# An agent attention with two expert layers: routing of a group may begin earlier, and the order's estimate counts SyncE's time differently

## The chip, the cores and the metric

The kernel runs on one core of one Trainium2 chip. The core has TensorE for matmuls (PE in the rows), VectorE (DVE), ScalarE (ACT), GpSimd (POOL) and SyncE (SP), which here issues nearly all transfers. The metric is the device time of one execution, in microseconds (us), as the median over runs.

## The reference

There are 2 batches of 11456 rows with 128 channels. First comes agent attention: 49 agents attend to all keys of their batch, which gives a table of agent values, and each row's query attends to the 49 agents. Then two layers of experts follow, each with 8 experts of which a row takes one:

```python
def sm(a, b):
    s = scale * (a @ b.transpose(0, 2, 1))
    e = np.exp(s - s.max(-1, keepdims=True))
    return e / (e.sum(-1, keepdims=True) + 1e-09)
x = (sm(q, agents) @ (sm(agents, k) @ v)).reshape(B * S, D)

# layer 1: logits of normalised rows against normalised embeddings, / tau
# layer 2: logits = x @ w_gate
for each layer:
    expert_idx = argmax(logits); gate_w = softmax(logits)[expert_idx]
    h = relu(x[mask] @ w1[e])                       # 128 -> 1024
    out[mask] = gate_w[mask, None] * (h @ w2[e])    # 1024 -> 128
```

## The kernel before, in words

**Groups and units.** The rows of a batch are cut into 12 groups, 11 of 1024 rows and one of 192, so there are 24 groups, numbered 0 to 23. In a group most rows take one expert, the dominant one. The group as a whole goes through the dominant expert of layer 1, then through the dominant expert of layer 2. Rows that want another expert go onto lists and are done after the groups. The work of one layer on 512 rows is a unit. A unit has 8 steps, one per 128 columns of the hidden layer. Units of layer 1 of group i alternate with units of layer 2 of group i - 2; steps are counted through all units.

**A step.** TensorE makes the first product into PSUM (h), ScalarE writes relu of it as a 16 bit value (hh), VectorE writes the remainder (hl), and TensorE adds the second product to acc. In layer 1 the first product is two matmuls, h<-pt,slotG, with weights (slotG) that already hold the agent values times the expert's first matrix; the second is acc<-hh,slot2a twice and acc<-hl,slot2a once. In layer 2 it is h<-yh,slot1b twice, h<-yl,slot1b once, and three of acc with slot2b. There are 4 buffers for h (NH), so TensorE may have up to three steps of first products ahead of the second products.

**Between the layers.** The result of layer 1, acc, is split into yh (ScalarE) and yl (VectorE), turned by a transpose transfer (yr) and written to DRAM (R). For a group's routing, the queries are loaded (qt), cast by ScalarE and split by GpSimd (qs), multiplied by the agents on TensorE, put through a softmax on VectorE and ScalarE (sd, pr) and turned by a transpose transfer (pt). Some twenty small VectorE operations (lg, lwq, lm, oh, key, md, dom, ks, di) find each row's expert and the number di of the dominant one. SyncE reads that number into a register (value_load, TENSOR_LOAD in the order) and loads the weights it names (slotG, slot2a, later slot1b, slot2b). In the second batch the attention is computed from kt and vb in the same stretches; ScalarE casts them to ws.

**What sets the order.** Each engine runs its instructions in a fixed order, written when the program is built. A planner walks through the steps; class Clock (line 88 on) holds an estimate of when each engine is free and each tensor is written. Method note (line 126) prices an instruction: for a transfer the engine's own time, then the time of SyncE's transfers in line (hw) and the arrival; for a value_load the engine's time. Work besides the steps comes from chains, generators that start at a given step with a priority: chain_Q loads the queries of a group, chain_A does its first routing, chain_B the second, chain_S2 loads slots, chain_Z writes out results. Where an engine has room by the estimate, the planner places the next piece of a chain; time_L1 and time_L2 (line 2030 on) say when a first or a second product could go, and the earlier one is issued. So an estimate that changes moves instructions on every engine, and the chip then runs that order with its own times. s1 of a group is the step of its first unit; for group 3 and later it is 64 + 32 (i - 3).

Of the kernel before, what the change touches and what calls it, by code (L numbers as in the profile page):

```python
# [84 lines left out]
class Clock:  # L85
# [38 lines left out]
    def note(self, k, op, a, kw):  # L124
        ap = lambda x: type(x).__name__ == "AP"
        out = kw.get("out", a[0] if a else None)
        ins = [x for i, x in list(enumerate(a[1:])) + list(kw.items()) if ap(x) and i not in ("out", "accum_out")]
        outs = [x for x in (out, kw.get("accum_out")) if ap(x)]
        name = lambda x: x.tensor.name
        loc = lambda x: x.space != bass.MemoryType.DRAM and not name(x).startswith(("Sbig", "LF1", "LF2"))  # L130
        s = max(self.t, self.eng[k])
        for x in ins:
            if loc(x) and name(x) in self.wr:
                e, q = self.wr[name(x)]
                s = max(s, e + self.LAG[q])
        for x in outs:
            if loc(x):
                s = max(s, self.rd.get(name(x), 0.0))
        if "dma" in op:
            e = s + (1.05 if k == "pool" else 1.17 if "transpose" in op else 0.06)  # L140
            nb = min(x.nbytes() for x in outs + ins[:1])
            if k != "pool":
                self.hw = max(self.hw, s) + 0.47
            self.dma = max(self.dma, (e if k == "pool" else self.hw) + 0.65) + nb / 300e3 * (0.3 if "cond" in kw else 1.0)
            self.arr = self.dma + 1.0
            for x in outs:
                if loc(x):
                    self.wr[name(x)] = (self.arr, "dma")
            for x in ins:
                if loc(x):  # L150
                    self.rd[name(x)] = self.arr
            self.eng[k] = e
            return
        if op == "value_load":
            self.eng[k] = s + 0.1
            return
        both = sum(ap(x) and x.space not in (PSUM, bass.MemoryType.DRAM) for x in [kw.get(n) for n in ("in_", "in0", "in1")])
        if k == "dve" and (both > 1 or both == 1 and op in ("tensor_scalar", "tensor_copy") and outs[0].size() // outs[0].shape[0] > 1):

            for a_, b_ in self.held:  # L160
                if a_ <= s < b_:
                    s = b_
        self.start = s
        e = s + (0.3 + 0.16 * (outs[0].size() // outs[0].shape[0]) if kw.get("op") == ALU.pow else self.price(k, op, outs[0] if outs else None, ins or outs, kw))
        if k == "pool" and both > 1 and kw.get("op") != ALU.pow:
            self.held = self.held[-12:] + [(s, e)]
        for x in outs:
            if loc(x):
                self.wr[name(x)] = (e, k)
        for x in ins:  # L170
            if loc(x):
                self.rd[name(x)] = max(e, self.rd.get(name(x), 0.0))
        self.eng[k] = e
        self.end = max(self.end, e)
# [24 lines left out]
def agent_moe_kernel(ctx, tc, qT, kT, v, agT, embT, tau, wg, w1a, w2a, w1b, w2b, cst, out):  # L199
    nc = tc.nc  # L200
    clk = Clock()
    pe, act, dve, pool, sp = (Queue(clk, k, e) for k, e in (("pe", nc.tensor), ("act", nc.scalar), ("dve", nc.vector), ("pool", nc.gpsimd), ("sp", nc.sync)))
# [677 lines left out]
    def until(*keys):  # L880
        yield keys
# [22 lines left out]
    def c_S(g):  # L904

        tp, nt = g.tp, g.nt
        if g.i >= 1:
            yield from until(("S", g.i - 1))
        if g.i >= NS:
            yield from until(("Sx", g.i - NS))  # L910
        if g.i >= NR:
            yield from until(("A", g.i - NR))
        qs = qsp.tile([128, 2048], F16, name="qs", tag="qs")
        ql = qs.bitcast(BF16)
        n = g.n
        act.activation(out=qs[:, 0:n], in_=g.q[:, 0:n], func=AF.Copy)
        yield 1
        pieces(ql[:, 1024:1024 + n], g.q[:, 0:n], qs[:, 0:n], ALU.subtract, 4)
        done.add(("qs", g.i))
        yield 1  # L920
        k = yield "m"
        psv = misc(k)[0:tp, 0:nt * A].rearrange("p (t a) -> p t a", a=A)
        for t in range(nt):
            scores(psv[:, t, :], qs[:, t * tp:(t + 1) * tp], ql[:, 1024 + t * tp:1024 + (t + 1) * tp], g.b)
        done.add(("S", g.i))
        yield 1
        mx = sm.tile([128, 8], F32, name="smx", tag="smx")
        dve.tensor_reduce(out=mx[0:tp, 0:nt], in_=psv, axis=AX, op=ALU.max)
        g.sd = sdp.tile([128, 8, A], F32, name="sd", tag="sd")
        sdv = g.sd[0:tp, 0:nt, :]  # L930
        dve.tensor_tensor(out=sdv, in0=psv, in1=b3(mx, g, A), op=ALU.subtract)
        free(k)
        yield 2
        act.activation(out=sdv, in_=sdv, func=AF.Exp, scale=isq, bias=ln64[0:tp])
        g.pr = prt[npr[0] % NR]
        npr[0] += 1
        pool.memset(g.pr[:, :, 49], 0.0)
        hi = g.pr.bitcast(F16)[0:tp, 0:nt, 0:A]
        act.activation(out=hi, in_=sdv, func=AF.Copy)
        yield 2  # L940
        pieces(g.pr.bitcast(F16)[0:tp, 0:nt, A:A2], sdv, hi, ALU.subtract, 2)
        done.add(("Sx", g.i))
        yield 2
# [182 lines left out]
    def chain_A(g):  # L1126

        b, tp, nt = g.b, g.tp, g.nt
        if g.i >= NS:
            yield from until(("A0", g.i - NS))  # L1130
        yield from until(("q", g.i), "S0", "setup")
        yield from c_S(g)
        if g.i >= NP:
            yield from reach(groups[g.i - NP].e1)
        yield from c_PT(g)
        yield 2
        yield from until(("av", b))
        if g.i:
            yield from until("crit")
        yield from c_X1(g)  # L1140
        yield 1
        yield from counts(g, g.oh, "1")
        sp.dma_start(out=nat(R1, g), in_=g.pr[0:tp, 0:nt, 0:PW])
        left = LF1[0:tp, b * NT + g.tile:b * NT + g.tile + nt, :]
        dve.tensor_tensor(out=left, in0=g.oh[0:tp, 0:nt], in1=g.dom[0:tp, None, :].to_broadcast([tp, nt, E]), op=ALU.is_gt)
        g.v1 = smg.tile([128, 8], F32, name="v1", tag="v1")
        vv = g.v1[0:tp, 0:nt]
        dve.tensor_reduce(out=vv, in_=left, axis=AX, op=ALU.add)
        dve.tensor_scalar(out=vv, in0=vv, scalar1=-1.0, scalar2=1.0, op0=ALU.mult, op1=ALU.add)
        done.add(("A0", g.i))  # L1150
        if g.i == 0:
            e = sp.value_load(g.di[0:1, 0:1], min_val=0, max_val=E - 1)
            yield from own("2a", e, slot2a[g.sl1], "x0")
            done.add("crit")
            prev["1", g.sl1] = e
            yield from until(*[("G", b, e_) for e_ in range(E)])
            slot_load("1g", g.sl1, e, [(slotG[g.sl1][0:A], one(Gsc, e)), (slotG[g.sl1][A:A2], one(Gsc, e))])
            done["w1", 0] = max(clk.arr, done["own", "2a"])
        yield from until(("K1", b))
        k1 = ksel(K1[:, b * E:(b + 1) * E], g.dom, "1")  # L1160
        g.f1 = smg.tile([128, 8], F32, name="f1", tag="f1")
        dve.tensor_scalar(out=g.f1[0:tp, 0:nt], in0=g.pr[0:tp, 0:nt, 49], scalar1=k1[0:tp], scalar2=None, op0=ALU.mult)
        done.add(("A", g.i))
        if g.i == 0:
            return
        yield from until(*[("G", b, e) for e in range(E)])
        yield ("us2", g.ready1)
        e = sp.value_load(g.di[0:1, 0:1], min_val=0, max_val=E - 1)
        r = e + b * E
        slot_load("1g", g.sl1, r, [(slotG[g.sl1][0:A], one(Gsc, r)), (slotG[g.sl1][A:A2], one(Gsc, r))])  # L1170
        yield from until(*[("2a", e_) for e_ in range(E)])
        slot_load("1", g.sl1, e, [(slot2a[g.sl1], one(Wsc["2a"], e))])
        done.arrives(("w1", g.i))
# [459 lines left out]
    def at(s, gen, pr=5):  # L1633

        waiting.append([s, 0.0, pr, len(waiting) + len(live), gen, None])
# [96 lines left out]
    with tc.manual_schedule():  # L1732
# [8 lines left out]
        for i in range(NG + LAG):  # L1741
            a = [(1, w) for w in groups[i].parts] if i < NG else []
# [4 lines left out]
            elif i == NG - 1:  # L1747
                a = []
# [10 lines left out]
        for u, (kd, w) in enumerate(seq):  # L1759
            g, o = w.g, order[kd]  # L1760
# [255 lines left out]
        at(0, filler(), 6)  # L2016
        for g in groups:
            at(max(0, g.s1 - 72), chain_Q(g), 0)
            at(max(0, g.s1 - 54), chain_A(g), 3 if g.i else 0)
            at(g.e1 + 4 if g.i else 0, chain_B(g), 3 if g.i else 0)  # L2020
            at(max(0, g.s2 - 12) if g.i else 0, chain_S2(g), 3 if g.i else 0)
        for u, w in kinds[2]:
# [180 lines left out]
```

## Time and profile before

| what | value |
|---|---|
| median of 3 runs | 1150.43 us (1147.48 to 1151.05) |
| profiled execution | 1146.86 us |
| its span | 1145.0 us |
| mean granted clock of TensorE | 0.962 |
| TensorE matmul busy | 1042.7 us (91%) |
| VectorE busy | 916.2 us (80%) |
| ScalarE busy | 659.7 us (58%) |
| GpSimd busy | 541.0 us (47%) |
| moved by DMA | 144.71 MB |

The busy share is a mean. The first 200 us, in which the attention of the first batch and the weights are made, have TensorE busy for 60.28 and 74.59 us of each 100; from 200 us on it is busy for 92.65 us and more of each 100. An idle engine costs time only where TensorE waits for it, so the pauses of TensorE are read one by one, with the engine or transfer that ended each.

### The profile page before, as it was taken

The numbers are of one execution on the slowest core, as the hardware profiler recorded it, in microseconds if no ns is written. First come the engines' busy times: TensorE is split into PE (matmuls) and PEld (weight loads), VectorE is DVE, ScalarE is ACT, GpSimd is POOL, SyncE is SP. The second block draws the span as 40 slices with busy tenths as digits, with TensorE's granted clock in tenths as the row PEclk, the third lists the DMA queues.
The fourth block names the chain that finished last, engine by engine and source line by source line (L and its number), as shares of the span: only waits on it lengthen the run. The fifth ranks groups of instructions, "written<-read, shape, count | busy, mean of one in ns | idle before, by whom it ended". The sixth has DMA issues, their size and how long they took to land. (4 is left out here: it accounts for less than half of the span.)

```text
span 1145.0 us, 22172 instructions
## 1 busy us (share of the span) xinstructions
PE 1042.7 (91%) x7147; PEld 529.7 (46%) x7232; DVE 916.2 (80%) x2557; ACT 659.7 (58%) x1172; POOL 541.0 (47%) x885
## 2 busy tenths in 40 slices
PE   4775677898999999999999899999999999999997
PEld 3633343454455455344454354444444444444544
DVE  6576989588888888967888988768788787887764
ACT  5435565676667665655655566555555656565543
POOL 1225655777776875344466432364644333322110
PEclk9875879999999999999999999999999999999999
DMA  9899989677555455744345453636245434322210
GB/s 317 229 289 293 260 275 218 178 151 122 122 114 113 105 116 104 155 103 81 88 73 92 100 130 68 120 65 144 50 100 117 87 68 82 78 56 67 56 37 34
DMA packets 243806, 144.71 MB, mean 126 GB/s; under 512 B 155160, under 2 KB 222042, under 8 KB 243682
## 3 DMA queue, kind: packets, MB, share of 16 engines
q1 hardware_dynamic: 240002, 141.80, 52.6%
q0 software_dynamic: 3680, 1.42, 0.8%
q8 instruction: 58, 0.95, 0.4%
q14 instruction: 66, 0.54, 0.2%
HBM read 108.05 MB, written 46.14 MB: 135 GB/s over the span
## 5 line engine op out<-in xcount | busy, mean ns | idle before, releaser
L193 ACT ACTIVATE hh<-h 128x512 f16<-128x512 f32 (+1 forms) x760 | 440.1, 585 | 350.3 <-PE h L193 308.8
L193 DVE SCALAR_TENSOR_TENSOR hl<-h,hh 128x512 bf16<-128x512 f32 (+1 forms) x760 | 498.1, 670 | 136.4 <-ACT hh L193 132.3
L193 PE MATMUL acc<-hh,slot2b 128*128 128x512 f16 (+1 forms) x784 | 229.9, 375 | 9.8 <-ACT hh L193 8.0
L193 PE MATMUL h<-yh,slot1b 128*128 128x512 f16 (+1 forms) x784 | 231.8, 377 | 3.9 <-DVE slot1b L193 2.1
L193 PE MATMUL h<-pt,slotG 98*128 98x512 f16 (+1 forms) x736 | 218.2, 379 | 2.6 <-DMA slotG<-Gsc 2.0
L193 PE MATMUL acc<-hh,slot2a 128*128 128x512 f16 (+1 forms) x736 | 215.3, 373 | 1.7 <-ACT hh L193 0.2
L193 PEld LDWEIGHTS <-slot1b 128*128 128x128 f16 (+1 forms) x1224 | 115.7, 99 | 144.2 <-issue 16.7
L193 PEld LDWEIGHTS <-slot2b 128*128 128x128 f16 (+1 forms) x1224 | 115.1, 98 | 139.4 <-issue 11.7
L193 PEld LDWEIGHTS <-slot2a 128*128 128x128 f16 x1104 | 104.3, 97 | 122.3 <-issue 4.7
L193 PE MATMUL acc<-hl,slot2b 128*128 128x512 bf16 (+1 forms) x389 | 145.8, 375 | 3.1 <-DVE hl L193 2.6
L193 PE MATMUL acc<-hl,slot2a 128*128 128x512 bf16 (+1 forms) x360 | 134.4, 373 | 8.8 <-DVE hl L193 8.6
L193 PE MATMUL h<-yl,slot1b 128*128 128x512 bf16 (+1 forms) x318 | 119.9, 377 | 0.0
L193 POOL DMA_INDIRECT L<-id,dsi x90 | 88.8, 987 | 50.7 <-issue 44.9
L193 PEld LDWEIGHTS <-slotG 98*128 98x128 f16 x736 | 68.8, 98 | 84.6 <-issue 13.0
L193 POOL TENSOR_TENSOR zo<-zr 128x256 f32<-128x256 f16 x86 | 56.1, 673 | 90.2 <-DMA zr<-zo 77.9
L193 POOL TENSOR_TENSOR qs<-qt,qs 128x256 bf16<-128x256 f32 (+1 forms) x96 | 59.4, 650 | 55.6 <-ACT qs L193 55.3
L193 POOL TENSOR_TENSOR zo<-zo 128x256 bf16<-128x256 f32 x86 | 56.1, 672 | 38.4 <-ACT zo L193 38.3
L193 POOL TENSOR_TENSOR fac<-fac,half 128x8 f32<-128x8 f32 (+1 forms) x24 | 38.7, 1614 | 51.2 <-DVE fac L193 50.6
L193 POOL TENSOR_TENSOR pr<-sd,pr 128x196 f16<-128x196 f32 (+1 forms) x48 | 24.2, 526 | 67.1 <-ACT pr L193 67.1
L193 POOL TENSOR_TENSOR zo<-zo,f 128x256 f32<-128x256 f32 x86 | 51.4, 617 | 0.2
L193 POOL TENSOR_TENSOR ws<-kt,ws 128x256 bf16<-128x256 f32 (+1 forms) x56 | 34.1, 639 | 9.0 <-DMA kt<-in_kT 8.7
L193 POOL TENSOR_TENSOR ws<-vb,ws 128x256 bf16<-128x256 f32 (+1 forms) x50 | 31.7, 665 | 13.4 <-ACT ws L193 13.3
(338 smaller groups left out, 1287.0 us busy)
## 6 DMA issues: line engine op xcount, KB each, us to landing
slot1b<-Wsc1b SPq DMA_DIRECT2D x26, 512.0 KB
slot2b<-Wsc2b SPq DMA_DIRECT2D x26, 512.0 KB
slot2a<-Wsc2a SPq DMA_DIRECT2D x23, 512.0 KB
R<-yr SPq DMA_DIRECT2D x22, 516.0 KB
qt<-in_qT SPq DMA_DIRECT2D x22, 512.0 KB
vb<-in_v SPq DMA_DIRECT2D x20, 512.0 KB
out<-zo SPq DMA_DIRECT2D x40, 256.0 KB
slotG<-Gsc SPq DMA_DIRECT2D x48, 196.0 KB
```

Of the source, the lines that this page charges most:

```text
L193: return f(*a, **kw)
```

## The change

It has three parts. In Clock.note a transfer that SyncE issues now takes 0.4 us of SyncE's estimated time (0.1 if it is conditional, 1.2 if it is a transpose; GpSimd's stays 1.05), and hw follows SyncE's end and has no 0.47 us per transfer of its own. A value_load in the estimate waits until the number has been written. And chain_A may start 72 steps in front of s1, as chain_Q does, where it was 54.

```diff
--- before.py
+++ after.py
@@ -137,10 +137,10 @@
             if loc(x):
                 s = max(s, self.rd.get(name(x), 0.0))
         if "dma" in op:
-            e = s + (1.05 if k == "pool" else 1.17 if "transpose" in op else 0.06)
+            e = s + (1.05 if k == "pool" else 1.2 if "transpose" in op else 0.1 if "cond" in kw else 0.4)
             nb = min(x.nbytes() for x in outs + ins[:1])
             if k != "pool":
-                self.hw = max(self.hw, s) + 0.47
+                self.hw = max(self.hw, e)
             self.dma = max(self.dma, (e if k == "pool" else self.hw) + 0.65) + nb / 300e3 * (0.3 if "cond" in kw else 1.0)
             self.arr = self.dma + 1.0
             for x in outs:
@@ -152,7 +152,8 @@
             self.eng[k] = e
             return
         if op == "value_load":
-            self.eng[k] = s + 0.1
+            e, q = self.wr.get(name(a[0]), (0.0, "dve"))
+            self.eng[k] = max(s, e + self.LAG[q]) + 0.1
             return
         both = sum(ap(x) and x.space not in (PSUM, bass.MemoryType.DRAM) for x in [kw.get(n) for n in ("in_", "in0", "in1")])
         if k == "dve" and (both > 1 or both == 1 and op in ("tensor_scalar", "tensor_copy") and outs[0].size() // outs[0].shape[0] > 1):
@@ -2016,7 +2017,7 @@
         at(0, filler(), 6)
         for g in groups:
             at(max(0, g.s1 - 72), chain_Q(g), 0)
-            at(max(0, g.s1 - 54), chain_A(g), 3 if g.i else 0)
+            at(max(0, g.s1 - 72), chain_A(g), 3 if g.i else 0)
             at(g.e1 + 4 if g.i else 0, chain_B(g), 3 if g.i else 0)
             at(max(0, g.s2 - 12) if g.i else 0, chain_S2(g), 3 if g.i else 0)
         for u, w in kinds[2]:
```

No instruction is added or removed by it on purpose; the estimates set another order. Three places of the new order follow.

SyncE around step 46, in before: the last transposes of yr, then a write, the reading of the number (TENSOR_LOAD), loads of weights for group 3 (slotG, slot2a), then the keys kt of the second batch.

```order
L193 DMA_TRANSPOSE yr<-yl 128x4x128
L193 DMA Wsc2b<-ws 128x2048
L193 DMA R_123<-pr_182 1024x1x50
L193 TENSOR_LOAD di_2792
...
L193 DMA slotG_172<-Gsc 49x2048
...
L193 DMA slotG_172<-Gsc 49x2048
...
L193 DMA slot2a_174<-Wsc2a 128x2048
L193 DMA kt<-in_kT 128x1024 x2
L193 DMA R_124<-yr 1024x1x129
```

The same place now:

```order
L194 DMA slot2a_174<-Wsc2a 128x2048
L194 DMA Wsc1b<-ws 128x2048
L194 DMA Wsc2b<-yd 128x2048
L194 DMA_TRANSPOSE yr<-yh 128x4x128
L194 DMA_TRANSPOSE yr<-yl 128x4x128
L194 DMA_TRANSPOSE yr<-yh 128x4x128
L194 DMA_TRANSPOSE yr<-yl 128x4x128
L194 DMA Wsc2b<-zo_180 128x2048
L194 DMA Wsc1b<-ws 128x2048
L194 DMA Wsc2b<-zo_179 128x2048
L194 DMA kt<-in_kT 128x1024 x2
```

The reading of the number and the loads of slotG and slot2a moved ahead of the four transposes, and writes of weights (Wsc) stand between the transposes and kt.

ScalarE at step 352, in before: after yh come lex, sd and pr of routing, then the hh of step 352 and on.

```order
L193 ACTIVATE hh<-h 128x512 x3
L193 ACTIVATE yh<-acc 128x512
L193 ACTIVATE lex_9984<-lg_9783 128x64
L193 ACTIVATE sd<-sd,ln_128 128x392
L193 ACTIVATE pr_184<-sd 128x8x49
```

The same place now:

```order
L194 ACTIVATE zo_179<-zo_179 128x512
L194 ACTIVATE hh<-h 128x512 x4
L194 ACTIVATE yh<-acc 128x512
L194 ACTIVATE hh<-h 128x512
L194 ACTIVATE lex_10048<-lg_9853 128x64
```

One hh moved ahead of lex, and sd and pr are no longer at this place.

TensorE at step 104, the first unit of a group's layer 2, in before: first products of the new unit (h, slot1b) alternate with second products of the old one (acc, slot2a); LDWEIGHTS loads the weights of the matmul behind it.

```order
L193 MATMUL acc<-hl,slot2a_173 128x512
L193 LDWEIGHTS slot1b_175
L193 MATMUL h<-yh,slot1b_175 128x512
L193 LDWEIGHTS slot1b_175
L193 MATMUL h<-yh,slot1b_175 128x512
L193 LDWEIGHTS slot1b_175
L193 MATMUL h<-yl,slot1b_175 128x512
L193 LDWEIGHTS slot2a_173
L193 MATMUL acc<-hh,slot2a_173 128x512
```

The same place now:

```order
L194 MATMUL acc<-hh,slot2a_173 128x512
L194 LDWEIGHTS slot2a_173
L194 MATMUL acc<-hl,slot2a_173 128x512
L194 LDWEIGHTS slot2a_173
L194 MATMUL acc<-hh,slot2a_173 128x512
L194 LDWEIGHTS slot2a_173
L194 MATMUL acc<-hh,slot2a_173 128x512
L194 LDWEIGHTS slot2a_173
L194 MATMUL acc<-hl,slot2a_173 128x512
L194 LDWEIGHTS ones_126
L194 MATMUL mi_4459<-oh_4130,ones_126 128x8
```

All second products of the old unit now stand ahead of the first h of the new one, with small products of routing (mi) between.

## Rows read from the trace of the kernel before

**Rows 1.** page part 5, one group: busy, mean, idle before and releaser

```profile
L193 PE MATMUL acc<-hh,slot2b 128*128 128x512 f16 (+1 forms) x784 | 229.9, 375 | 9.8 <-ACT hh L193 8.0
```

**Rows 2.** TensorE's timeline: start, us, operation, in brackets idle before it and releaser

```profile
151.88 1.44 PE L193 MATMUL h<-pt,slotG 98*128 98x512 f16 x3 [2.04 <-DMA slotG<-Gsc]
...
191.48 0.61 PE L193 MATMUL h<-yh,slot1b 128*128 128x512 f16 x1 [2.09 <-DVE slot1b L193]
...
207.80 0.59 PE L193 MATMUL acc<-hh,slot2b 128*128 128x512 f16 x2 [3.22 <-ACT hh L193]
...
635.71 1.01 PE L193 MATMUL acc<-hh,slot2b 128*128 128x512 f16 x2 [4.20 <-ACT hh L193]
```

**Rows 3.** 4 us windows: busy of each engine, granted clock, DMA share, GB/s

```profile
204.00:208.00 4.00, 0.78 (x4) 0.28 (x3) 0.21 (x1) 2.85 (x4) 2.08 (x4) 1.00 1.13 275
...
208.00:212.00 4.00, 3.87 (x33) 1.92 (x31) 2.96 (x5) 3.33 (x7) 3.85 (x7) 0.57 0.92 247
...
632.00:636.00 4.00, 0.29 (x1) 0.10 (x1) 3.52 (x16) 2.24 (x5) 2.82 (x5) 0.89 0.18 67
...
636.00:640.00 4.00, 4.00 (x14) 1.52 (x13) 3.91 (x8) 1.82 (x5) 1.95 (x4) 0.68 0.01 0
```

**Rows 4.** ScalarE's timeline at step 46

```profile
204.79 1.06 ACT L193 ACTIVATE ws<-kt 128x1024 f16<-128x1024 f32 x1 [5.13 <-DMA kt<-in_kT]
```

**Rows 5.** SyncE's timeline: the issues ahead of kt, and a pt transpose

```profile
153.44 3.58 SPq L193 DMA_TRANSPOSE pt<-pr  x1
...
190.60 4.38 SPq L193 DMA_TRANSPOSE yr<-yl  x1
...
195.08 0.53 SPq L193 DMA_DIRECT2D Wsc2b<-ws  x1
...
198.16 0.56 SPq L193 DMA_DIRECT2D slotG<-Gsc  x2
...
199.25 0.83 SPq L193 DMA_DIRECT2D kt<-in_kT  x2
```

**Rows 6.** ScalarE's timeline at step 352

```profile
632.65 0.26 ACT L193 ACTIVATE lex<-lg 128x64 f32<-128x64 f32 x1 [4.22 <-DVE lg L193]
```

**Rows 7.** VectorE's timeline at step 352

```profile
628.57 0.23 DVE L193 TENSOR_TENSOR lg<-lg,fac 128x64 f32<-128x64 f32 x1
...
629.56 3.06 DVE L193 TENSOR_TENSOR lg<-lg,lmx 128x64 f32<-128x64 f32 x1
```

**Rows 8.** GpSimd's timeline at step 352, first and last pair of the run

```profile
628.85 1.29 POOL L193 TENSOR_TENSOR zo<-zo 128x256 bf16<-128x256 f32 x2
...
631.36 1.18 POOL L193 TENSOR_TENSOR zo<-zo,f 128x256 f32<-128x256 f32 x2
```

**Rows 9.** TensorE's timeline at first units of a second layer

```profile
241.20 0.22 PE L193 MATMUL mi<-agh,ws 128*128 128x49 f16 x2 [0.30 <-POOL ws L193]
...
334.24 0.38 PE L193 MATMUL acc<-hl,slot2a 128*128 128x512 bf16 x1 [0.82 <-DVE hl L193]
...
381.53 0.38 PE L193 MATMUL acc<-hl,slot2a 128*128 128x512 bf16 x1 [0.95 <-DVE hl L193]
...
385.08 0.59 PE L193 MATMUL acc<-hh,slot2b 128*128 128x512 f16 x2 [0.59 <-ACT hh L193]
...
593.64 0.24 PE L193 MATMUL acc<-hl,slot2a 128*128 128x192 bf16 x1 [0.71 <-DVE hl L193]
...
595.27 0.24 PE L193 MATMUL acc<-hl,slot2a 128*128 128x192 bf16 x1 [0.44 <-DVE hl L193]
...
770.43 0.59 PE L193 MATMUL h<-yh,slot1b 128*128 128x512 f16 x2
...
825.15 0.38 PE L193 MATMUL acc<-hl,slot2b 128*128 128x512 bf16 x1 [0.81 <-DVE hl L193]
```

**Rows 10.** SyncE's timeline, the issue of a q load

```profile
836.11 0.57 SPq L193 DMA_DIRECT2D qt<-in_qT  x1
```

**Rows 11.** ScalarE's timeline, the cast of that load

```profile
852.92 1.05 ACT L193 ACTIVATE qs<-qt 128x1024 f16<-128x1024 f32 x1
```

## The prediction

> **What bounds the kernel now.** I read the busy shares on the page first, then the costliest groups, then TensorE's timeline for its pauses, then short windows for its granted clock, and last the timelines of the engines that a pause names.
>
> The reader is to see that TensorE is the bound and has little left to give back. From about 220 us it pauses rarely, and the pauses are single events, not a steady loss. In the group acc<-hh,slot2b, TensorE idles 9.8 us over the whole run, 8.0 us of it for ScalarE's hh [rows 1]. Two pauses make 7.42 us of those 8.0: 3.22 us ending at 207.80, and 4.20 us ending at 635.71 [rows 2]. I call them E (step 46) and J (step 352). Each is followed by a stretch at a lower clock. The 4 us after E were granted 0.57 and those after J 0.68; the stretches of the pauses themselves had 1.00 and 0.89 [rows 3]. A shortened pause may also save matmul time that runs at the lower of the two levels (1.2 GHz against 2.4).
>
> So the question is not how much work is saved, but which of these pauses the new order removes, and which it makes.
>
> **The change part by part.** It adds no operation: both orders hold the same matmuls. Three numbers steer the planner; what they do is seen in the order alone. Routing of a group (chain_A) stands 10 to 18 steps earlier. In before it was ready some 31 steps ahead of its unit, and the one long wait of TensorE for a slot of weights that it chose is that at group 1 [rows 2]. I cost the shift itself at nothing, with those 31 steps as its cover; what it moves besides is costed next.
>
> *E.* ScalarE stood idle 5.13 us for a transfer of kt, and every hh after it waited, at 204.79 [rows 4]. SyncE had issued that kt at 199.25. In front of it stood the last yr transpose (till 194.98), Wsc2b, R<-pr, a wait for the expert number, and two slotG loads at 198.16 [rows 5]. In the new order (first pair of excerpts) the number and the slot loads stand ahead of the transposes, and kt comes after four transposes and three 0.5 us writes. 194.98 + 3 x 0.53 = 196.6, so about 2.6 us before 199.25, with the transposes where they were. kt then lands at 204.79 - 2.6 = 202.2. One cast of 1.06 us, not two, stands ahead of the next hh, which is free at 203.3. TensorE wanted it at 207.80 - 3.22 = 204.58. The pause goes whole: 3.22, and with it 4 x (1 - 0.57) = 1.72 of clock. **E is -4.9.** Lower bound: if the landing is set by what the transfers move, and not by when SyncE issues them, 0. What is late next is the second cast, which now has its own hh in front.
>
> *Opening of group 1.* One pt transpose is moved ahead of the slot loads of group 1. In before such a transpose took SyncE 3.58 us at 153.44 [rows 5], and TensorE had waited 2.04 us for slotG [rows 2]. The waiting matmul at 151.88 is one that nothing covers. One transpose ahead costs up to 3.58; a Wsc2b write of some 0.53 us that goes behind is taken off; the wait for the number, which would be spent anyway, absorbs more. I take 0 and keep -2.0 to +2.4.
>
> *Step 40.* TensorE waited 2.09 us for slot1b, at 191.48 [rows 2]. Five small VectorE operations of routing leave the place before it, but yl and lg, lwq, lm, oh remain, and the two inv0 now stand behind yl, so ScalarE's half of slot1b begins later. I take 0, from -1.0 (five operations at about the 0.2 of [rows 7]) to +0.5.
>
> *J.* ScalarE idled 4.22 us at 632.65 for lg, with four hh behind it [rows 6], and lg had waited on VectorE: 3.06 us for an operation that took 0.23 us a microsecond earlier [rows 7]. GpSimd ran tensor_tensors without a break from 628.85 to 632.54 [rows 8]. In the new order (second pair) hh stands ahead of lex, so ScalarE no longer waits. But 17 small operations still stand between yl and the next hl on VectorE. At 0.2 each they end at 629.6 + 3.4 = 633.0, hl at 633.7; TensorE has its two acc<-hh done at 631.5 + 0.4. The pause is 1.7 instead of 4.2: -2.5, and -0.6 to -1.3 of clock (4 x (1 - 0.68) = 1.28). That is -3.1 to -3.8 if VectorE runs free. If it is held until 632.54 again, nine operations and hl follow: 632.5 + 1.8 + 0.7 = 635.0, gain 1.2. GpSimd's run at that place grows in the order from six to ten tensor_tensors; if VectorE is held through 10 x 0.62 instead of 6 x 0.62, J is 2.5 worse than before. **I take -3.0**, near the free end, because the nearest row, at 628.57 beside the same GpSimd, shows 0.23.
>
> A rule of the Trainium skill speaks against this term: in "SBUF — State Buffer", section "SBUF: two separate sides", GpSimd and VectorE share one port pair that is locked by whichever starts first, for a whole instruction, and a VectorE operation with two SBUF inputs then stands still. The row of 3.06 us, which ends as GpSimd's run ends, agrees. By that rule alone J would be -1.2 and my sum 1.8 higher. The free rows beside it are why I don't take it for the value.
>
> *Drained boundaries.* At the first unit of a group's second layer TensorE may have up to three steps of first-layer products in hand, or none (third pair of excerpts: all second-layer products first, then the new h). With none, it waits for ScalarE and VectorE at the next hh or hl. Seven places are new in the order: steps 72, 104, 136, 200, 296, 328, 448. Before shows the price at three such places: 0.95 + 0.59 = 1.54 at 381 to 385, nothing at 770, 0.81 at 825 [rows 9]. The mean is 0.78, times 7 is 5.5. What TensorE paused at the same places in before goes: two of 0.30 at 241, 0.82 at 334, 0.71 + 0.44 at 594 and 595 [rows 9], together 2.57. **+2.9**, from -2.6 (no cost) to 7 x 1.54 - 2.57 = +8.2.
>
> *A cast beside its load.* qs<-qt stood at least 16 us behind its load in the second half (852.92 against 836.11 [rows 10, 11]). In the new order some ten of them stand only 6 to 9 steps behind the earliest place of the load. A step is (635 - 204) / 306 = 1.4 us, so 8.5 to 12.7 us of cover, against the 5.5 us that kt took (204.79 - 199.25). It covers the load if SyncE issues in time. If not, ScalarE blocks every hh, as at E: 3.22 + 1.72 = 4.9 each. I take a quarter of one pause, **+0.8**, from 0 to +9.8 (two).
>
> **Sum.** -4.9 - 3.0 + 2.9 + 0.8 = -4.2. The profiled execution was 1146.86 (span 1145.0 and 1.9 around it), so 1142.7. The median of the runs shown is 1150.43, 3.6 above, so the forecast in its terms is **1146.2 us**. Its own range, with J between -3.8 and -1.2 and the drains between -2.6 and +8.2, is 1140 to 1153.
>
> **Rivals.**
> - *It only moves* (same). E's kt lands no earlier: what speaks for it is that the DMA share of 204 to 208 was 1.13 [rows 3]; against, that its slotG loads are out of the way. Then E is 0, and the sum is -3.0 + 2.9 + 0.8 = +0.7: 1151.1. VectorE held at J alone gives -2.4: 1148.0, also within what can be told.
> - *ScalarE waits for a load with hh queued behind it* (slower). The mechanism of E, at the qs casts. With one such wait the sum is -4.2 - 0.8 + 4.9 = -0.1; it decides from the second on: +4.8, 1155.2. Three give 1160. For it: the shorter cover, and that ScalarE takes its work in order. Against: 8.5 us is still over 5.5, and the DMA is idler after 220.
> - *The drains are dear* (slower or same): all seven at 1.54 and J held, -4.9 - 1.2 + 8.2 + 0.8 = +2.9, 1153.3.
> - *The change does nothing*: the routing was early enough, and E and J are accidents of one order that others replace: 1150. What speaks for it is that all steady stretches are full; it goes with the first.
>
> **Chances.** Forecast 0.43; it only moves or does nothing 0.30; casts that wait 0.17; dear drains, with other trouble, 0.10. About 0.3% (3.45 us) is what a measurement here can tell from no change: under 1147.0 is faster, over 1153.9 slower. Most of the forecast's own chance lies below 1147.0, the rest is made up by cases of the rivals in which E and the drains both go well: faster 0.43, same 0.31, slower 0.26. The 8-in-10 range runs from 1139 (drains cost nothing, E whole, J free: -4.9 - 3.8 - 2.6 + 0 = -11.3) to 1159 (between two and three waiting casts).
>
> **What would show it.** E right: no pause of over 1 us near 205, kt landing before 203, clock 1.00 after it. J right: ScalarE without a wait at step 352, a pause below 2 us for hl. Drains right: pauses for hl or hh of 0.5 to 1.6 us at about half of the seven steps. Casts: no ScalarE wait for qt. The forecast is wrong if qs or ws waits over 4 us for a transfer with hh behind it, if group 1 opens over 2 us later, or if a new pause above 3 us stands anywhere after 220.

## The result and the profile after

The changed kernel took 1160.83 us (median of 4, 1157.82 to 1164.51) beside 1150.45 us for the kernel before: a ratio of 1.0101, 95% interval 1.0070 to 1.0132. It is slower by 1.0%, where 0.4% faster was forecast, and the time lies above the stated range (1139 to 1159). The profiled execution took 1157.82 us, span 1156.0, clock 0.961; that of before had a span of 1145.0. TensorE's matmuls were busy for 6.6 us more (1049.3 instead of 1042.7), so some 4.4 us of the 11 are longer idle time.

Where the 11 us lie is seen by setting the two traces side by side. The table gives the start of ScalarE's hh of a step, which both kernels do in the same order:

| step | before us | changed us | change since the line above |
|---|---|---|---|
| 32 | 173.8 | 171.4 | -2.4 |
| 48 | 209.2 | 204.8 | -2.1 |
| 160 | 368.2 | 366.2 | +2.4 |
| 192 | 414.1 | 421.0 | +9.0 |
| 344 | 616.7 | 626.4 | +2.8 |
| 360 | 643.8 | 655.1 | +1.6 |
| 528 | 852.4 | 866.2 | +2.5 |
| end of span | 1145.0 | 1156.0 | -2.8 |

One stretch, steps 160 to 192, makes most of it. Part 5 of the profile shows the kind of loss. Beside [rows 1], where acc<-hh,slot2b had idled 9.8 us, the changed kernel's page has, with the same columns:

```profile
L194 PE MATMUL acc<-hh,slot2b 128*128 128x512 f16 (+1 forms) x784 | 230.4, 375 | 4.2 <-ACT hh L194 4.2
...
L194 PE MATMUL acc<-hl,slot2b 128*128 128x512 bf16 (+1 forms) x392 | 147.4, 376 | 22.9 <-DVE hl L194 22.0
```

The wait for ScalarE's hh is halved, as forecast. The idle time of the matmuls with VectorE's hl on the same tile is now 22.9 us. On the page of before that group had 3.1:

```profile
L193 PE MATMUL acc<-hl,slot2b 128*128 128x512 bf16 (+1 forms) x389 | 145.8, 375 | 3.1 <-DVE hl L193 2.6
```

TensorE's timeline of the changed kernel (idle before it and releaser in brackets) has these pauses where [rows 2] and [rows 9] had theirs, and new ones:

```profile
149.40 1.01 PE L194 MATMUL h<-pt,slotG 98*128 98x512 f16 x2 [3.60 <-DMA slotG<-Gsc]
...
181.49 0.82 PE L194 MATMUL mi<-slot1b 128*128 128x128 bf16 x6 [3.58 <-DMA slot1b<-in_w1b]
...
194.12 0.39 PE L194 MATMUL h<-yh,slot1b 128*128 128x512 f16 x1 [1.05 <-DVE slot1b L194]
...
227.78 0.38 PE L194 MATMUL acc<-hl,slot2b 128*128 128x512 bf16 x1 [4.14 <-DVE hl L194]
...
249.18 0.38 PE L194 MATMUL acc<-hl,slot2b 128*128 128x512 bf16 x1 [0.89 <-DVE hl L194]
...
337.60 0.59 PE L194 MATMUL acc<-hh,slot2b 128*128 128x512 f16 x2 [1.59 <-ACT hh L194]
...
376.41 0.58 PE L194 MATMUL acc<-hl,slot2b 128*128 128x512 bf16 x1 [7.64 <-DVE hl L194]
...
645.90 0.59 PE L194 MATMUL acc<-hl,slot2b 128*128 128x512 bf16 x1 [5.68 <-DVE hl L194]
...
853.81 0.59 PE L194 MATMUL acc<-hh,slot2a 128*128 128x512 f16 x2 [1.42 <-ACT hh L194]
```

Three pauses, 4.14, 7.64 and 5.68 us, end with hl. VectorE's timeline shows what it did instead, where [rows 7] had one such row:

```profile
219.75 5.63 DVE L194 TENSOR_SCALAR f<-fg,kr 128x8 f32<-128x8 f32 x1
...
364.67 0.28 DVE L194 TENSOR_REDUCE lg<-mi 128x64 f32<-128x128 f32 x1
364.99 10.52 DVE L194 TENSOR_TENSOR lg<-lg,fk 128x64 f32<-128x64 f32 x1
375.54 0.22 DVE L194 TENSOR_REDUCE lmx<-lg 128x8 f32<-128x64 f32 x1
375.68 0.68 DVE L194 SCALAR_TENSOR_TENSOR hl<-h,hh 128x512 bf16<-128x512 f32 x1
...
636.35 3.67 DVE L194 SCALAR_TENSOR_TENSOR fac<-sP,c,fac 128x8 f32<-128x8 f32 x1 [0.64 <-POOL fac L194]
```

Three of these rows are long: f, lg<-lg,fk and fac. Each is a small operation of routing, with a median of 0.2 to 0.4 us in this trace, and the next hl stands behind it on VectorE. GpSimd's timeline beside the longest, as [rows 8] beside the 3.06 us of before:

```profile
365.04 1.04 POOL L194 TENSOR_TENSOR es<-Sbig,es 128x196 f16<-128x196 f32 x2
366.04 2.55 POOL L194 TENSOR_TENSOR ws<-vb,ws 128x256 bf16<-128x256 f32 x4
368.55 1.28 POOL L194 TENSOR_TENSOR zo<-zr 128x256 f32<-128x256 f16 x2
369.81 2.54 POOL L194 TENSOR_TENSOR ws<-vb,ws 128x256 bf16<-128x256 f32 x4
372.31 2.54 POOL L194 TENSOR_TENSOR qs<-qt,qs 128x256 bf16<-128x256 f32 x4
374.82 1.18 POOL L194 TENSOR_TENSOR zo<-zo,f 128x256 f32<-128x256 f32 x2
```

GpSimd ran tensor_tensors without a gap from 365.04 to 376.00, and VectorE stood from 364.99 to 375.51, through 17 of them. I call that a hold. The clock adds to the pause, as in [rows 3] (columns as there; the first row stands behind the pause of 4.14 us at 224):

```profile
228.00:232.00 4.00, 4.00 (x27) 1.78 (x26) 2.87 (x7) 2.28 (x4) 1.40 (x3) 0.57 0.63 167
...
368.00:372.00 4.00, 0.77 (x4) 0.25 (x3) 4.00 (x1) 1.68 (x3) 4.00 (x7) 0.99 0.01 2
372.00:376.00 4.00, 0.00 (x0) 0.00 (x0) 3.97 (x3) 0.00 (x0) 4.00 (x7) 0.50 0.00 0
376.00:380.00 4.00, 3.59 (x9) 1.25 (x9) 3.79 (x16) 1.45 (x3) 0.04 (x1) 0.50 0.00 0
380.00:384.00 4.00, 4.00 (x26) 2.46 (x25) 3.16 (x10) 1.86 (x4) 1.97 (x5) 0.73 0.17 35
```

The granted clock was 0.50 in the last 4 us of the pause of 7.64 us. Behind it TensorE worked at 1.2 GHz (0.50) until 380, and at a mean of 0.73 for another 4 us.

### The profile page after: what moved, and what is told of

It reads as the page before. It is cut to its first block, busy times and chain, and to the rows that moved or that the text cites. A ratio compares the mean times of both kernels' runs of the same rounds, so it can differ in the third digit from the quotient of the medians.

```text
span 1156.0 us, 22249 instructions
## 1 busy us (share of the span) xinstructions
PE 1049.3 (91%) x7232; PEld 530.4 (46%) x7232; DVE 922.1 (80%) x2557; ACT 660.4 (57%) x1172; POOL 532.4 (46%) x869
## 3 DMA queue, kind: packets, MB, share of 16 engines
q0 software_dynamic: 3680, 1.42, 0.8%
## 4 chain that ended last, share of the span: by engine, by line
PE 69%; DVE 17%; DMA 6%; issue 3%; ACT 2%; POOL 1%; SPq 0%; DVEq 0%; ACTq 0%; POOLq 0%
PE acc L194 34%; PE h L194 30%; PE mi L194 5%; DVE hl L194 5%; DVE lg L194 2%; DVE fac L194 1%; DMA qt<-in_qT 1%; ACT hh L194 1%; DMA slot1b<-in_w1b 1%; DVE ws L194 1%; DMA R<-pr 1%; DVE f L194 1%; DMA wl<-in_w1a 1%; DVE yl L194 1%; DMA kt<-in_w2a 1%
## 5 line engine op out<-in xcount | busy, mean ns | idle before, releaser
L194 PEld LDWEIGHTS <-slot1b 128*128 128x128 f16 (+1 forms) x1232 | 115.5, 98 | 152.9 <-issue 23.7
L194 PE MATMUL acc<-hl,slot2b 128*128 128x512 bf16 (+1 forms) x392 | 147.4, 376 | 22.9 <-DVE hl L194 22.0
L194 PE MATMUL h<-yl,slot1b 128*128 128x512 bf16 (+1 forms) x392 | 147.7, 377 | 0.0
L194 PE MATMUL acc<-hl,slot2a 128*128 128x512 bf16 (+1 forms) x368 | 137.7, 374 | 4.5 <-DVE hl L194 4.2
L194 POOL DMA_INDIRECT L<-id,dsi x90 | 91.9, 1021 | 45.7 <-issue 36.1
L194 POOL TENSOR_TENSOR qs<-qt,qs 128x256 bf16<-128x256 f32 (+1 forms) x96 | 58.4, 641 | 64.6 <-ACT qs L194 49.6
L194 ACT ACTIVATE zo<-acc 128x512 f32<-128x512 f32 (+1 forms) x49 | 28.7, 586 | 17.8 <-PE acc L194 15.0
L194 ACT ACTIVATE yh<-acc 128x512 f16<-128x512 f32 (+1 forms) x46 | 26.9, 584 | 20.4 <-PE acc L194 15.9
```

The source lines that it names most:

```text
L194: return f(*a, **kw)
```

## The experiments

Theory H: holds of VectorE by GpSimd's runs make the difference; the new order has more of them in front of an hl. Rivals: D, drained units; P, the new estimate itself; S, the order is worse in other ways; G, GpSimd's speed; L, that the order of before is a good draw and most others lose. Times are medians; ratios are to the kernel before in the same batch of runs. Hold sums count what VectorE's operations took over their usual time (the median of the same operation in the trace), after 200 us, where that is over 1 us: 12.7 us in before, 25.2 in the changed kernel.

**Each part alone.** The value_load line moves nothing: with that line alone, the built order equals that of before row for row, and the estimate without it gives the same order as with it. Two parts are left.

```diff
-            at(max(0, g.s1 - 54), chain_A(g), 3 if g.i else 0)
+            at(max(0, g.s1 - 72), chain_A(g), 3 if g.i else 0)     # e1 alone
# e2: the hunks of Clock.note alone, chain_A at 54
```

> The kernel before with chain_A at 72 steps as its one change. Theory H (VectorE is held through a whole run of GpSimd tensor_tensors, and a new order makes such holds by chance): 1145 to 1160 us, with pauses of TensorE over 3 us each standing beside a VectorE operation of over 2 us, wherever they fall; the summed excess of held VectorE operations over 1 us (10 us in before, 20 us in the changed kernel, after 200 us) tells the time. Rival D (early routing drains TensorE at the first units of a second layer): 1156 to 1160 us, lost in pieces of 0.5 to 1.6 us at seven steps. Rival P (the new estimate is what harms): within 3 us of 1150.

> The kernel before with the estimate of SyncE's time and the wait of value_load changed, chain_A at 54. Theory H: 1145 to 1160 us, the time told by where holds fall. Rival D: within 3 us of 1150, since routing doesn't begin earlier. Rival P: 1157 to 1162 us, as the changed kernel.

e1 took 1163.35 us (1.0111, 1.0080 to 1.0141), more than H or D had allowed (1160), and e2 1157.27 (1.0054, 1.0035 to 1.0074). Each half loses alone: P falls with e1, which has nothing of the new estimate, and D as the whole cause with e2, which loses without earlier routing. The hold sums are 16.5 and 19.3, the smaller one in the slower kernel, so the sum doesn't tell the time as H had it. e1 also has a pause of 6.03 us for a transfer:

```profile
609.88 0.23 PE L193 MATMUL mi<-Rh,pt 98*128 98x58 f16 x1 [6.03 <-DMA pt<-pr]
```

In e2 the two pauses of over 4 us (second fence, TensorE) end behind holds of 5.46 and 5.51 us (first fence, VectorE):

```profile
417.01 5.46 DVE L194 SCALAR_TENSOR_TENSOR lwq<-lg,cs 128x64 f32<-128x64 f32 x1
...
770.45 5.51 DVE L194 TENSOR_SCALAR f<-pr,kr 128x8 f32<-128x8 f32 x1
```

```profile
423.30 0.96 PE L194 MATMUL mi<-ws,es 128*98 128x129 f16 x7 [4.59 <-DVE lg L194]
...
776.61 0.59 PE L194 MATMUL acc<-hl,slot2a 128*128 128x512 bf16 x1 [4.10 <-DVE hl L194]
```

**A memset between GpSimd's operations.**

```diff
-            return f(*a, **kw)
+            r = f(*a, **kw)
+            if k == "pool" and op == "tensor_tensor" and Queue.gap is not None:
+                eng.memset(Queue.gap, 0.5)       # one column of a constant
+            return r
```

> The changed kernel, with a memset of one column (about 0.1 us) behind each of GpSimd's tensor_tensors, nothing else moved. Theory H: the memset lets VectorE in, as it seemed to at 632.5 us of before, so the holds of 10.5, 5.6 and 3.7 us shrink under 1.5 us; the pauses of 7.64, 4.14 and most of 5.68 us go, and the time falls by 10 to 16 us to 1145 to 1151. If a memset doesn't free VectorE, or holds are not the cause: 1158 to 1164, GpSimd's runs being a few us longer. Rivals D and P: no gain, 1158 to 1164.

> The kernel before with the same memsets. Theory H: the hold of 3.06 us at 629.6 and those of 2.3 to 3.9 us elsewhere go, of which only the first stands before a pause; 3 to 6 us faster, 1144 to 1148. Rivals D and P: 1149 to 1153.

e3 took 1158.49 us (1.0091, 1.0062 to 1.0121), e4 1167.37 (1.0148, 1.0120 to 1.0175). The expectation failed: a memset doesn't let VectorE in. e3's hold sum did fall, to 11.5, with other operations held than in the changed kernel, and the time hardly followed. In e4 the same f that had stood for 2.55 us in before stood 11.77 us, through 18 tensor_tensors and the memsets between them. The cause is not refuted by it, the remedy is: e4 got slower with a hold sum of 25.9. That the memset at 632.5 of before had released VectorE isn't shown.

```profile
415.81 11.77 DVE L195 TENSOR_SCALAR f<-fg,kr 128x8 f32<-128x8 f32 x1
```

**GpSimd without its reads.** The order of the other engines stays; the remainders and the outputs are left out.

```diff
+            if Queue.blank:                       # set inside pieces()
+                return eng.memset(kw["out"], 0.0) # e13: two of them
             return f(*a, **kw)
```

> The changed kernel, in which each of GpSimd's large tensor_tensors (remainders ws, qs, es, pr, zo and the products of the output) is a memset of the same output: the remainders and the outputs are left out, the order of every other instruction stays. Theory H (holds of VectorE by GpSimd's runs make the difference): no VectorE operation is held over 1 us, the pauses at 369 (7.64), 224 (4.14) and 640 (5.68) shrink under 1.5 us, and this kernel and the next, the one before with the same edit, come within 3 us of each other. Rival S (the order is worse by itself, at drained units, late loads of weights and casts): this kernel stays 7 to 11 us behind the next.

> The kernel before with the same edit. Theory H: 1140 to 1147 us, the pause of 4.20 at 631 gone. Rival S: the same, since before lost little to holds; the difference to the changed kernel with the same edit is what tells.

> As the changed kernel without GpSimd's reads, but each large tensor_tensor is two memsets of its output, so that GpSimd is about as long busy (some 0.55 us each instead of 0.27; a tensor_tensor took 0.65). The remainders are left out as there. Theory H (holds of VectorE by GpSimd's reads): operations of VectorE with two operands are still never held; 1134 to 1144 us against 1150 of before. Rival G (GpSimd's earlier end was the gain): 1152 to 1161.

e5 took 1135.91 us (0.9877, 0.9812 to 0.9942), e6 1143.28 (0.9917, 0.9881 to 0.9953), e13 1131.58 (0.9841, 0.9800 to 0.9881). The changed order gains 25 us by it, that of before 8, and it is then the faster one by some 7 us, which speaks against S. That is more than H expected (within 3 us). In e6 the pause of 4.20 us at J is not gone but 2.46. e13 keeps GpSimd busy for 494 us, e5 for 326, and e13 is not slower, so GpSimd's shorter busy time was not the gain. G isn't ruled out whole by it: a memset reads nothing and so doesn't wait for its input (GpSimd's qs waited 49.6 us for ScalarE's qs in the changed kernel, in e5 and e13 not at all). The drains below settle that. In e13 no operation of VectorE is held over 1 us.

In e5 VectorE still is held over 1 us in eleven stretches, some 30 us together and no less than in the changed kernel, where H had expected none. Yet no pause for hl is over 2.15 us in it, so what a hold costs depends on where it falls. Each of these stretches begins with a tensor_scalar beside a run of memsets, none with an operation of two operands. VectorE, then GpSimd:

```profile
223.15 3.91 DVE L198 TENSOR_SCALAR f<-fg,kr 128x8 f32<-128x8 f32 x1
```

```profile
222.91 0.58 POOL L197 MEMSET zo<- 128x256 bf16 x2
223.41 2.10 POOL L197 MEMSET ws<- 128x256 bf16 x8
225.44 1.09 POOL L197 MEMSET qs<- 128x256 bf16 x4
```

The same f in e13, and GpSimd beside it:

```profile
221.72 0.23 DVE L199 TENSOR_SCALAR f<-fg,kr 128x8 f32<-128x8 f32 x1
```

```profile
221.61 0.32 POOL L197 MEMSET zo<- 128x256 bf16 x1
221.99 0.31 POOL L198 MEMSET zo<- 128x256 bf16 x1
222.24 0.31 POOL L197 MEMSET ws<- 128x256 bf16 x1
222.61 0.31 POOL L198 MEMSET ws<- 128x256 bf16 x1
```

In the rows of e5 each memset starts some 0.07 us before the one ahead of it has ended. In e13 the second of a pair starts 0.06 us after the first has ended (222.55 to 222.61). Some 90 tensor_scalars of VectorE start beside a memset there, and none takes over 0.5 us.

The Trainium skill, in "SBUF — State Buffer", section "SBUF: two separate sides", says that an operation of VectorE with two SBUF operands competes only with a GpSimd operation that reads SBUF, while one in a 2-port performance mode competes with any. The holds of e5 agree; that its tensor_scalars run in such a mode, no trace here shows. It also says that the lock is held for the whole instruction. The rows above show a longer wait: 10.52 us is some 17 instructions of 0.63.

**Changes without meaning.**

```diff
-            at(max(0, g.s1 - 54), chain_A(g), 3 if g.i else 0)
+            at(max(0, g.s1 - 55), chain_A(g), 3 if g.i else 0)     # e7
-    HOP = 0.2
+    HOP = 0.21                                                     # e8
```

> The kernel before with chain_A at 55 steps instead of 54: no meaning of its own, but some thousands of rows of the order move. Theory L (the order of before is a good draw, and nearly any other order loses several us to holds and late arrivals that the planner doesn't see): 1154 to 1163 us. Rival M (the loss comes from what the change means, routing 18 steps early and SyncE's price): within 3 us of 1150.5.

> The kernel before with the planner's hop between engines at 0.21 us instead of 0.20, nothing else: again a meaningless change that moves thousands of rows. Theory L: 1154 to 1163 us, with pauses at other places than before. Rival M: within 3 us of 1150.5.

e7 took 1160.92 us (1.0080, 1.0035 to 1.0126), e8 1165.37 (1.0115, 1.0084 to 1.0146). L holds in both (e8 lies 2 us above its range), M falls: one step or 0.01 us costs as much as the change. Their hold sums are 21.6 and 23.7. The longest in e8, and the pause behind it:

```profile
321.73 8.75 DVE L193 SCALAR_TENSOR_TENSOR fac<-sP,c,fac 128x8 f32<-128x8 f32 x1 [0.20 <-POOL fac L193]
```

```profile
332.28 0.58 PE L193 MATMUL acc<-hl,slot2b 128*128 128x512 bf16 x1 [7.88 <-DVE hl L193]
```

**A drain behind each tensor_tensor.**

```diff
+            if k == "pool" and op == "tensor_tensor":
+                eng.drain()
```

> The changed kernel with a drain (an instruction that waits until the engine has finished) behind each of GpSimd's tensor_tensors; all computation and the order of every other instruction stay. Theory H: a drain leaves a gap in GpSimd's runs in which a held VectorE operation gets in, so no hold lasts longer than one tensor_tensor (0.65 us), the pauses at 369, 224 and 640 go, and the time falls to 1138 to 1148 us. If a hold doesn't end in such a gap: 1158 to 1166. Rival G (what helped with memsets was that GpSimd finished earlier, 326 us busy instead of 532): a drain makes GpSimd slower, so 1160 to 1170.

> The kernel before with the same drains. Theory H: 1141 to 1148 us, within some 4 us of the changed kernel with drains, which by the run without GpSimd's reads is the faster of the two. Rival G: 1151 to 1160.

> The kernel with the planner's hop at 0.21 us (1165 us without drains) and the same drains. Theory H with L: the draws differ mostly in which VectorE operations are held, so with drains this one comes down by 12 to 22 us, to 1143 to 1153. Rival G or a bad order by itself: 1160 to 1172.

> The changed kernel once more, for a second profile. If a hold follows from the order alone, the same VectorE operations are held as in the first profile (f at 220, lg at 365, fac at 636, each over 3 us). If it is a matter of nanoseconds where they meet GpSimd, other operations are held, or the same ones for other lengths, and the time differs by some us, as the runs' range of 1158 to 1165 suggests.

In this batch the kernel before itself took 1187.15 us instead of 1151, so only ratios and the traces are used. e9 had 1.0092 (1.0060 to 1.0124), e10 1.0121 (1.0050 to 1.0192), e11 1.0140 (1.0075 to 1.0204). No hold was left over 1 us in any of the three, as H expected, but the time didn't fall: GpSimd now is late, and TensorE waited 7.38 us for its qs in e9 and 16.37 for its oh in e11. By their ratios (on 1151 us some 1162 and 1167) e9 and e11 lie where G had put them, and e10 (1165) above that. e12, the changed kernel as it is, took 1185.08 us in its one execution, no more than before in that batch, with lg<-lg,fk at 0.64 us and no hold above 2.9. It decides nothing by itself, but it goes with H: without the long holds the changed kernel was not behind.

**A drain behind each group of two or four.**

```diff
             if c.stop > c.start:
                 pool.tensor_tensor(out=out[:, c], in0=in0[:, c], in1=in1[:, c], op=op)
+        nc.gpsimd.drain()          # e14, e15; e17, e18: only if clk.eng["pe"] > 200.0
```

> The changed kernel with one drain behind each group of two or four tensor_tensors instead of behind each one: less time lost on GpSimd. Theory H: a hold may last one group, 1.3 to 2.6 us, and not longer; the time lies 3 to 9 us under the changed kernel's of the same chip. If drains cost what they give: within 3 us of it, or above.

> The kernel before with the same drains. Theory H: within 3 us of before, which has one long hold to lose (4.2 us at 631) and little else; the gap to the changed kernel with drains closes to under 4 us. Rival S (the changed order is worse in itself): the gap stays 7 us or more.

> The changed kernel once more, timed and with a profile, on the chip and in the time of the three kernels above. Theory H with chance in it: 1156 to 1165 us, ratio 1.004 to 1.014, with holds over 2 us at other places than in the first profile, or of other lengths. If holds follow from the order alone: f at 220, lg at 365 and fac at 636 again, 4 to 10 us each.

e16, the changed kernel again, took 1165.37 us (1.0126, 1.0079 to 1.0173). With the drains, e14 took 1150.06 (0.9986, 0.9960 to 1.0011): 15 us less, more than the 3 to 9 expected. Before with drains, e15, took 1158.33 (1.0063, 1.0028 to 1.0098), 8 us more than e14 and 7 more than before, where H had it within 3: the drains cost that order more than they gave. With holds cut short (hold sums 2.7 and 2.2), the changed order is ahead, so S falls. e14 computes all that e16 does, in the same order on every engine, and its GpSimd is busy for 538 us, e16's for 532; so G falls too.

The traces place what each edit took from the changed order (differences of the profiled spans in us, each pair from one batch except e5's):

| steps | held there in the changed kernel | e14 less e16 | e13 less e16 | e5 less the changed kernel |
|---|---|---|---|---|
| 48 to 72 | f, 5.63 | -6.7 | -7.2 | -4.3 |
| 160 to 176 | lg, 10.52 | -10.8 | -11.2 | -10.2 |
| 344 to 360 | fac, 3.67 | -1.2 | -5.9 | -6.4 |
| all others | | +0.5 | -9.9 | -0.3 |
| span | | -18.2 | -34.3 | -21.1 |

The gain of the drains lies at the holds of f and lg, and nowhere else on balance: 17.5 of 18.2 us.

e16's profile answers whether holds fall by chance. VectorE, then TensorE:

```profile
224.92 5.62 DVE L194 TENSOR_SCALAR f<-fg,kr 128x8 f32<-128x8 f32 x1
...
370.77 10.52 DVE L194 TENSOR_TENSOR lg<-lg,fk 128x64 f32<-128x64 f32 x1
...
644.15 3.67 DVE L194 SCALAR_TENSOR_TENSOR fac<-sP,c,fac 128x8 f32<-128x8 f32 x1 [0.64 <-POOL fac L194]
```

```profile
382.19 0.58 PE L194 MATMUL acc<-hl,slot2b 128*128 128x512 bf16 x1 [7.64 <-DVE hl L194]
```

The same operations are held for the same lengths (5.62, 10.52, 3.67), 5 to 8 us later in the run than in the first profile. So a hold belongs to the order as long as the engines' timing stays as it is; e12, the same program in the slower batch, had none of the three. In these two executions the chance that I had assumed is in the order and not in the execution.

**Fewer drains.**

> The changed kernel with a drain behind each group of GpSimd's tensor_tensors, but only from 200 us of the planner's time on (241 drains, 25 fewer): in the profile of the kernel with all of them, TensorE waited 4.20 us for GpSimd's qs at 194, which the changed kernel without drains does not. Theory H: that wait goes and the holds stay short, 1143 to 1149 us, the first kernel here under before. If the wait only moves: 1148 to 1153.

> The same drains in the kernel with the estimate changed and chain_A at 54 (1157 us without drains). Theory H: its holds of 4.7 to 5.3 us at 363, 417 and 770 go, of which two stand before pauses of 4.6 and 4.1: 1146 to 1152 us. If its loss lies elsewhere: 1154 to 1160.

e17 took 1150.04 us (0.9989, 0.9961 to 1.0018), e18 1155.46 (1.0025, 0.9998 to 1.0051). In e17 the wait for qs at 194 went, but f, now without a drain in front, was held again, 5.61 us at 222, and the pause of 4.40 us came back. The gain and the loss are equal. e18's holds of 5 us went (hold sum 1.2), but its time lies where the loss is elsewhere (1154 to 1160), and its ratio is no clear step from e2's 1.0054: the intervals overlap, and GpSimd's oh, late by 3.38 us at 792, is new. No kernel here that computes the whole result beats the kernel before beyond its interval.

## Why the prediction was wrong, point by point

- **E (-4.9): right in its place.** SyncE issued kt at 193.58, not 2.6 but 5.7 us earlier than in [rows 5]: the transposes ahead of it ended at 190.24 and not at 194.98, and the three writes took 3.2 us and not 1.6. ScalarE's cast had no wait before it (compare [rows 4]), and no pause of TensorE stands near 205:

```profile
201.58 1.05 ACT L194 ACTIVATE ws<-kt 128x1024 f16<-128x1024 f32 x1
202.53 0.59 ACT L194 ACTIVATE hh<-h 128x512 f16<-128x512 f32 x1
```

  Steps 40 to 48 became 6.8 us shorter. But in the 8 steps ahead of them TensorE waited 3.58 us for weights (slot1b<-in_w1b, above). The prediction had not looked for that wait; net of it, steps 32 to 48 gained 2.1 us.
- **Group 1 (0, to +2.4): inside.** Its wait grew from 2.04 to 3.60.
- **Step 40 (0): better**, 1.05 instead of 2.09.
- **J (-3.0): failed.** ScalarE indeed waited no longer. VectorE was held, and earlier than I had looked: in fac, 3.67 us, ahead of yl. The pause was 5.68, against 1.7 forecast for VectorE running free, 3.0 for it held until GpSimd's run of before had ended, and 6.7 for it held through all ten operations. I had named the last case and left it out of the range. In e13, which has no holds, the pause is 1.88, so the free case was sized rightly. With drains (e14) it is still 3.91, since fac and three operations behind it each wait out an operation or two of GpSimd.

```profile
622.65 0.38 PE L199 MATMUL acc<-hl,slot2b 128*128 128x512 bf16 x1 [1.88 <-DVE hl L199]
```

- **Drained boundaries (5.5 for the seven): right.** They paused 0.53 + 0.89, 0, 1.59, 0.54 + 0.62, 0, 0.30 and 0, together 4.5.
- **Casts (+0.8): the wait came, its price didn't.** ScalarE waited for qt four times in the second half, 2.01 to 3.92 us, where before never did [rows 11]; only the last shows on TensorE as more than 1 us, 1.42 at 853.81.

```profile
803.88 1.06 ACT L194 ACTIVATE qs<-qt 128x1024 f16<-128x1024 f32 x1 [3.43 <-DMA qt<-in_qT]
...
852.22 1.06 ACT L194 ACTIVATE qs<-qt 128x1024 f16<-128x1024 f32 x1 [3.92 <-DMA qt<-in_qT]
```

- **The step that failed** is "I cost the shift itself at nothing, with those 31 steps as its cover": the sum has a term for a held VectorE at J and none anywhere else. The cover is true for TensorE's waits on slots. But a new order, whether from the shift (e1) or from the estimate (e2), moves VectorE's small operations against GpSimd's runs, and each meeting may hold an hl behind it. I had the row (3.06 us, [rows 7]) and the rule, and asked about them at one place only. The two new holds, at 220 and 365, cost 4.14 + 7.64 us of pause and, by an estimate from the windows above, some 4.6 us of clock (3.59 us of matmuls at 0.50 and 4 us at 0.73 make 1.8 + 1.1; 4 us at 0.57 after the pause at 224 make 1.7). That is 16.4 us, more than the whole 11, and the drains took 17.5 us away at the same two places (e14 less e16). The rest of the order gained, as forecast: with the holds cut or moved the changed order is ahead of that of before by 7 to 8 us (e5 against e6, e14 against e15).
- A fourth hold, fac at 829.85 for 2.91 us, stands ahead of a pause of 1.83 us for hh at 835.59, which is counted in none of these terms.
- None of the four rivals had this cause. The prediction's own sign of being wrong, a new pause above 3 us after 220, came three times.
- I also priced a hold by a neighbouring row in which it didn't happen (0.23). A wait that comes or stays away should have been priced at both ends, with even weight, at every place.

What ends a hold, the traces show in part. Beside the longest one each of GpSimd's operations starts some 0.03 us before the one ahead of it has ended, and so do e4's memsets (0.05 us). The hold of fac, 636.35 to 640.02, ended where GpSimd's run has a gap of 0.10 us:

```profile
638.82 1.18 POOL L194 TENSOR_TENSOR zo<-zo,f 128x256 f32<-128x256 f32 x2
640.10 1.29 POOL L194 TENSOR_TENSOR zo<-zr 128x256 f32<-128x256 f16 x2
```

After 200 us, in no run here does an operation of VectorE that is held over 1 us stay held across a gap of more than 0.02 us between GpSimd's tensor_tensors and memsets, and most holds end with the run or while its last operation goes on. The gaps of 0.06 us in e13 and of 0.16 us behind the drains of e9 and e14 fit. The profile's ends of GpSimd's operations are rough, and no run varied the gap alone, so this is a reading and not shown as the cause.

What stays open: why some holds end in the middle of a run (in the changed kernel those of 1.33 and 1.58 us at 317 and 424), and why many operations that start beside a run are not held at all, as the 0.23 us of [rows 7]. Which are held is fixed by the order and shifts with the timing of the engines (e3 and e12 have none of the three long holds of e16). The planner's estimate does let a VectorE operation wait for a GpSimd operation under way (the list held in Clock), at its own estimated times; no run here tests that part.

## What to carry to other kernels

Where two engines can hold each other, a reordered schedule is a new draw: compare its gain with the spread of meaningless reorderings (here +0.8% and +1.15% from one step and 0.01 us), before asking what the change means. Don't go by the sum of holds: e1 with 16.5 us of them was no faster than the changed kernel with 25.2. Look in the trace for small operations that take many times their usual length, and at what stands behind them on their engine; price them at every place where the order moves such an operation beside a run of the other engine, above all where that other engine's result releases it (fac after GpSimd's fac) and its next operation starts at the same moment. A bare drain between such runs can be worth it (15 us in e14). It can also cost more than it gives, where the drained engine comes late (e9 to e11) or the order had few holds to lose (7 us in e15).

## What the runs showed of the hardware that was not expected

- VectorE stood 10.52 us in one operation of 0.2 us, through 17 back-to-back operations of GpSimd, and 11.77 us in e4 through 18 with a memset of 0.1 us behind each. Drains behind groups kept all holds under 1.8 us in e14 and under 1.4 us in e15.
- A gap of 0.06 us between two memsets (e13) or of 0.10 us between two tensor_tensors (at 640 of the changed kernel) went with a VectorE that was not held, or no longer; after 200 us no hold over 1 us in any run spans a gap of more than 0.02 us.
- The lengths of holds repeat to 0.01 us between executions in two batches of runs (5.63 and 5.62, 10.52 twice, 3.67 twice); in a third batch (e12) the three were not there.
- The granted clock was 0.50 in the last 4 us of a pause of 7.64 us and in the 4 us behind it, and 0.73 in the next 4.
